# Three second-layer products of two units taken by a second level of fast products, and the order of the additions around them

## The chip, the cores and the metric

The kernel runs on one core of a Trainium2 chip. Its time is the device time of one execution in microseconds (us); the time before is the median of three executions, 630.69 us (630.52 to 631.08). The profile is of one more execution, and a profile starts at that execution's first instruction: places such as "at 597.34" are microseconds from there.

The engines are named as the profile names them. PE (TensorE) multiplies; PEld is its loading of weights. DVE (VectorE) and POOL (GpSimd) add and subtract, ACT (ScalarE) copies out of the accumulators and applies the activation, SP (SyncE) issues transfers. [...]

## The reference

A recurrent attention block gives 3072 tokens of 512 numbers; a two-layer network with a leaky activation follows. The second part is what matters here:

```python
def _moe_ref(x, w_in, w_out) -> np.ndarray:     # x 3072x512, w_in 512x2048, w_out 2048x512
    h = x @ w_in
    g = np.maximum(0.01 * h, h)
    return (g @ w_out).astype(np.float32)
```

Everything is float32. One product of the program is two matmul records in the profile[...].

## The kernel before

Tokens are worked in six chunks of 512 (c = 0 to 5), the 2048 hidden numbers in four units of 512 (u = 0 to 3). One step of the main loop is one unit of one chunk: n = 4(c - 2) + u runs from 0 to 15, and n = 12 to 15 are the last chunk. The first two chunks are done earlier, in another way.

Both layers use fast matrix products of the Strassen-Winograd kind. A 512x512 by 512x512 product is cut into 2x2 blocks and needs seven block products instead of eight, for a price of block sums before and after. "By two levels" means that each of the seven is cut again in the same way: seven products of quarter blocks instead of eight. The seven products of a block, each with half the columns, are PE work; the sums of operands and of results are DVE, POOL and ACT work.

Each step n does, in this order on PE:

1. `inner(n+1, 0)`: four of the seven first-layer products of the **next** unit, by two levels (28 products of 128x128, L1390). ACT copies results out of the accumulators (L1394 to L1402), DVE adds the others (`plus`, L619).
2. `trunk(n)`: three of the seven second-layer products of this unit, by one level only: "A" from block g0, "C" and "B" from differences of g, four products of 128x256 each (L1351). All three are accumulated **in PSUM** over the four units of a chunk, in banks 5, 7 and 4; `first` says when an accumulation starts anew (at u = 0).
3. `inner(n+1, 1)`: the other three first-layer products, by two levels (21 products of 128x128, L1390, in banks 0 to 3).
4. `leaf_steps(n)`: the other four second-layer products of this unit, by two levels (28 products of 128x128, L1311, in banks 0, 1, 2 and 6).

Around this lie the sums. `differences` (L622, four subtractions of 128x512 on DVE) makes the block differences of g for the second layer. `outer` combines the first-layer results to g (five additions of 128x512 in its second part), and `leaky` (L1432, ACT) activates them. `leaf_sums(n)` (L1290) makes the second-level operands of the four leaf blocks, four POOL instructions of 128x512. The results of `leaf_steps` go into the tile `w5` (`leaf_rooms()[5]`), or straight into the output tile `o` when u = 0, and `add_results` adds `w5` to `o` later: one DVE addition of 128x2048. When the trunk's accumulation is complete (last unit of a chunk), `trunk_taken` copies bank "A" into **the same tile** `w5` (ACT, L1359) and DVE adds "B", "C" and the sums to `o`. In the last chunk this happens at n = 14, because n = 15 uses `output` instead (L674), one level for all seven.

The order is written by hand. In step n the DVE queue gets, in this order: `add_results`, `differences(n)`, the result sums of `inner(n+1, 0)`, the first two additions of `outer(n+1)`, the trunk sums if there are any, the result sums of `inner(n+1, 1)`, the other additions of `outer(n+1)`, the result sums of `leaf_steps(n)`. The ACT queue at n = 14 gets the five copies of `inner(15, 0)`, then the copy L1359 of `trunk_taken`, then the five copies of `inner(15, 1)`.

How `inner` uses banks matters below: its products M1, M5, M4, M6 go to banks 0, 1, 2 and 3. M6 adds to the result of M1, which ACT first copies from bank 0 to bank 3 (L1394), so that M6, the fourth group, cannot start before that copy. `leaf_steps` has the same copy (L1315) with one group less between: there M2, the third group, reuses the bank that the copy reads.

Of the kernel before, what the change touches and what calls it, by code (L numbers as in the profile page):

```python
# [9 lines left out]
FP32 = mybir.dt.float32  # L10
# [6 lines left out]
ALU = mybir.AluOpType  # L17
# [5 lines left out]
def kernel(  # L23
# [56 lines left out]
    def unit(k):  # L80
        if k not in units:
            units[k] = unit_tile(k, f"w{k}")
        return units[k]
# [121 lines left out]
    def new_t(c, name):  # L205
        return work.tile([128, 3, 2, N], FP32, tag=f"t{c % 2}", name=name)

    def new_o(c, name="o"):
        return work.tile([128, 4, 2, N], FP32, tag=f"o{int(c > 0)}", name=f"{name}_{c}")
# [408 lines left out]
    def plus(out, a, b):  # L618
        return nc.vector.tensor_tensor(out=out, in0=a, in1=b, op=ALU.add)  # L619
# [186 lines left out]
    def tile_x(c):  # L806
        return work.tile([128, 4, 2, N], FP32, tag="x", bufs=2, name=f"x_{c}")
# [3 lines left out]
        return [x, new_t(c, f"t_{c}")]  # L811

    slot = [0]
    last_four = {}

    class Reversed:

# [6 lines left out]
    def new_g(c, u):  # L824
        i = slot[0]
        slot[0] = 1 - i
        both = work.tile([128, 7, 2, N], FP32, tag=f"g{i}", name=f"g_{c}_{u}")
        last_four[c, u] = both[:, 1:5]
        return u, both[:, 0:4], Reversed(both)

    def run(steps, at):
# [240 lines left out]
    def at_of(n):  # L1072
        return 2 + n // NU, n % NU
# [121 lines left out]
    def flat_of(part):  # L1195
        return part.rearrange("p i k n -> p (i k n)")
# [106 lines left out]

    def leaf_steps(n, moving):

        ps = [bank[i].rearrange("p (i n) -> p i n", i=4) for i in (0, 2, 1, 6)]
        results = leaf_results(n)
        leaf_weights[:] = of_unit.pop(n, leaf_weights)
        for m, q, j, s in LEAVES:
            for i, to in enumerate(TARGETS):  # L1310
                nc.tensor.matmul(ps[q][:, to], lhsT=leaf_weights[i][j], rhs=moving[s][:, i],  # L1311
                                 start=(i == 0 and m in ("M1", "M5", "M4")), stop=True,
                                 skip_group_check=True)
            if m == "M1":
                nc.scalar.copy(out=ps[3], in_=ps[0])  # L1315
            elif m == "M3":
                plus(results[:, :, 1], results[:, :, 1], ps[1])
            elif m == "M7":
                plus(results[:, :, 3], results[:, :, 3], ps[3])
            else:  # L1320
                nc.scalar.copy(out=results[:, :, {"M5": 3, "M4": 2, "M6": 1, "M2": 0}[m]],
                               in_=ps[q])
            yield

        plus(results[:, :, 2], results[:, :, 2], ps[3])
        plus(results[:, 2], results[:, 2], results[:, 3])
        if at_of(n)[1] > 0:
            unadded.append(lambda: plus(flat_of(os[at_of(n)[0]]), flat_of(os[at_of(n)[0]]),
                                        results.rearrange("p i q n -> p (i q n)")))

    unadded = []

# [11 lines left out]
    def trunk(n, part):  # L1344

        u, g, gd = part
        first = n == FIRST_LEAVES or u == 0
        for x, sa, rhs in (("A", 0, g[:, 0]), ("C", 4, gd[:, 0]), ("B", 5, gd[:, 1])):
            for i in range(2):
                for k in range(2):  # L1350
                    nc.tensor.matmul(room[x][:, i, :],  # L1351
                                     lhsT=block(2 * u + 1, sa)[:, k, ts(i, 128)],
                                     rhs=rhs[:, k, :], start=(first and i == 0 and k == 0),
                                     stop=(k == 1), skip_group_check=True)
# [61 lines left out]
    def outer(n, group, later=None):  # L1416

        if group == 0:
            gs[n] = new_g(*at_of(n))
        g = gs[n][1]  # L1420

        def to(i):
            return g[:, i].rearrange("p k (h n) -> p (k h) n", h=2)

        def leaky(i):
            if later is not None:
                later.append(lambda: leaky_now(i))
            else:
                leaky_now(i)

        def leaky_now(i):
            nc.scalar.activation(g[:, i], g[:, i], AF.Prelu, alpha=0.01)  # L1432

        if group == 0:
            plus(u2, u2, m1)
            return plus(to(1), u2, m5)
        plus(to(0), m1, m2)
        leaky(0)
        plus(to(1), to(1), m3)
        leaky(1)  # L1440
        plus(u2, u2, m7)
        plus(to(3), u2, m5)
        leaky(3)
        plus(to(2), u2, m4)
        leaky(2)

    def products(steps, n):

        for _ in range(n):
            next(steps, None)  # L1450
# [38 lines left out]
    for n in range(N2):  # L1489
        c, u = at_of(n)  # L1490
        more, visiting, leaves = n + 1 < N2, visits(n), by_leaves(n)
        scores_next = visiting and following(c + 1, 2 * u)
        last_leaves = leaves and (u == NU - 1 or n + 2 == N2)
        if u == 0 and not leaves:
            os[c] = new_o(c)
        if u > 0:
            add_results()
        if more:
            differences(*gs[n][1:])
            if n > 0:  # L1500
                begun = inner_steps(n + 1, 0, held=visiting)
                products(begun, 1)
            while held:
                held.pop()()
            products(begun, 7)
        part = gs.pop(n)
        behind = None
        if visiting:
            if u == 0:
                xs[c + 1] = new_x(c + 1)  # L1510
            joint_visit(c + 1, 2 * u)
            if leaves:
                load_rows(n, range(4)[2 if u == 0 else 0 :])
        elif leaves and u == NU - 1:
            behind = sums_of_x(c + 1, 1)
        if more:
            outer(n + 1, 0)
        if leaves and u == 0:
            finish_chunk(c - 1)
            os[c] = new_o(c)  # L1520
        if visiting and u == 1:
            behind = differences(*xs[c + 1])
        elif c + 1 < NC and u == 2:
            behind = sums_of_x(c + 1, 0)
        if leaves:
            moving = leaf_sums(n, behind if not scores_next else None)
            trunk(n, part)
            if visiting and not scores_next:
                fill(6, 2, start=False)
        else:  # L1530
            steps = output(c, os[c], [part], u == 0, u == NU - 1, room=room if more else last_room,
                           order=FUSED if more else LAST, held=held if more else None)
            products(steps, 3)
        if last_leaves:
            rest = trunk_taken(n, os[c])
            if n + 2 == N2:
                rest()
        if scores_next and leaves:
            scores_of_pair(*scores_next, [bank[i] for i in (1, 6, 2, 3)], second_mask_last=True)
        elif scores_next:  # L1540
            scores_of_pair(*scores_next)
        if visiting:
            load_unit(n + 2, 0)
        if not leaves:
            products(steps, 1)
        if n in (0, 1):
            keep.append(sums_of_rows(n))
        if n in (1, 2):
            keep.append(sums_of_rows(n + 1, nc.gpsimd))
        if more:  # L1550
            inner(n + 1, 1)
            if last_leaves and n + 2 < N2:
                rest()
            for i in range(2) if visiting else ():
                ahead(c + 2, 2 * u + i)
            if keep:
                keep.pop(0)()
            if not leaves:
                products(steps, 1)
            later = [] if leaves else None  # L1560
            outer(n + 1, 1, later)
        if leaves:
            leaf = leaf_steps(n, moving)
            last_one = n + 2 == N2
            for count, ready in ((1, 1), (1, 1), (2, 2)) if last_one else (
                    (4, 2 if u == NU - 1 else 3), (1, 2 if u == NU - 1 else 1)):
                products(leaf, count)
                for _ in range(ready):
                    later.pop(0)()
            if last_one:  # L1570
                differences(*gs[n + 1][1:])
            products(leaf, 8)
            if last_one:
                add_results()
        else:
            products(steps, 3)
        if by_leaves(n + 1) and n + 1 >= NU:
            if not visits(n + 1):
                load_rows(n + 1)
            elif u == NU - 1:  # L1580
                load_rows(n + 1, range(2))
# [92 lines left out]
```

## Time and profile before

| what | us | from |
|---|---|---|
| median of three executions | 630.69 | times |
| the profiled execution | 631.22 | times |
| its span, first to last instruction | 629.3 | page |
| PE busy | 622.8 (99%) | page, part 1 |
| DVE busy | 512.4 (81%) | page, part 1 |
| ACT busy | 281.4 (45%) | page, part 1 |
| POOL busy | 105.8 (17%) | page, part 1 |
| step n = 12 | 546.27 to 568.67 | timeline of PE |
| step n = 13 | 568.67 to 591.08 | timeline of PE |
| step n = 14 | 591.08 to 613.49 | timeline of PE |

The profiled execution took 631.22 us, 1.9 us more than its span; that difference lies outside the first and last instruction. It is 0.5 us above the median.

In the timeline a row is a run of like instructions: its start, how long it lasted, engine, line, operation, tiles written and read with their shapes, how many, and in brackets the engine's idle time before it and what ended that. A duration holds whatever the instruction waited for inside the engine, so the same shape can have different durations. In the names, the free blocks of the weight tiles are all called `w`: `w<-bank` at L1359 is the trunk copy into `w5`.

### The profile page before, as it was taken

Reading aid. Unit: us, or ns where it says so; the run is one execution under the profiler, and the core shown is the slowest. Engines: PE = TensorE matmul, PEld = TensorE weight load, DVE = VectorE, ACT = ScalarE, POOL = GpSimd, SP = SyncE. Lnnn points to the kernel's source line nnn. Section 1 sums busy time; section 2 is a strip of 40 time slices with the busy share of each in tenths; the row PEclk is TensorE's granted clock in tenths of the full one; section 3 lists DMA queues with packets and bytes.
Section 4 is the critical chain, followed back from the end, with each engine's and each line's share of the span. In section 5 each row is a group of like instructions: output and inputs, shape, how many; then the busy total and the mean of one; then the engine's idle time right before and its main releaser. Section 6 shows DMA issues by size and latency. Waiting matters only on the chain.

```text
span 629.3 us, 15220 instructions
## 1 busy us (share of the span) xinstructions
PE 622.8 (99%) x6375; PEld 572.2 (91%) x6375; DVE 512.4 (81%) x793; ACT 281.4 (45%) x543; POOL 105.8 (17%) x109
## 2 busy tenths in 40 slices
PE   8999999999999999999999999999999999999997
PEld 5888888888888889899999999999999999999996
DVE  5679769889979986679888968789968689977796
ACT  5876646446444114352433433534514435534540
POOL 2000000000010110105133052331250321333030
PEclk9999999999999999999999999999999999999999
DMA  8941425547782998396976996988478568678601
GB/s 328 405 143 34 126 75 193 167 133 252 243 296 73 347 333 272 101 339 190 349 228 215 283 333 240 324 280 280 150 257 298 156 216 281 209 264 278 205 1 68
DMA packets 105939, 140.99 MB, mean 224 GB/s; under 512 B 4488, under 2 KB 84232, under 8 KB 105872
## 3 DMA queue, kind: packets, MB, share of 16 engines
q1 hardware_dynamic: 105568, 139.41, 66.6%
q8 instruction: 50, 0.82, 0.5%
q10 hardware_dynamic: 304, 0.62, 0.3%
q14 instruction: 17, 0.14, 0.1%
HBM read 113.54 MB, written 26.48 MB: 222 GB/s over the span
## 4 chain that ended last, share of the span: by engine, by line
PE 94%; DVE 2%; ACT 1%; DMA 1%; issue 0%; SPq 0%; DVEq 0%; ACTq 0%
PE bank L1390 27%; PE bank L1311 12%; PE bank L1351 10%; PE bank L674 9%; PE C_h L674 4%; PE B_o L674 4%; PE A_h L674 4%; PE A_o L674 4%; PE C_o L674 4%; PE B_h L674 4%; PE D_o L674 2%; PE D_h L674 2%; PE d L695 2%; DMA raw<-in_weights_dram 1%; PE bank L371 1%; PE bank L453 1%
## 5 line engine op out<-in xcount | busy, mean ns | idle before, releaser
L619 DVE TENSOR_TENSOR made<-made,bank 128x512 f32<-128x512 f32 (+1 forms) x96 | 55.9, 617 | 39.8 <-PE bank L1390 35.9
L1390 PEld LDWEIGHTS bank<-x,wb 128*128 128x128 f32 x672 | 77.4, 192 | 1.2 <-ACT bank L1394 0.2
L1390 PE MATMUL bank<-x,wb 128*128 128x128 f32 x672 | 78.4, 276 | 0.0
L622 DVE TENSOR_TENSOR g<-g 128x512 f32<-128x512 f32 x96 | 64.0, 688 | 5.2 <-ACT g L1432 0.5
L1390 PE MATMUL bank<-x,wa 128*128 128x128 f32 x512 | 67.7, 275 | 0.0
L1394 ACT COPY bank<-bank 128x512 f32<-128x512 f32 (+1 forms) x32 | 16.6, 517 | 104.6 <-PE bank L1390 97.4
L1390 PEld LDWEIGHTS bank<-x,wa 128*128 128x128 f32 x512 | 62.7, 192 | 0.5 <-ACT made L1400 0.2
L1390 PE MATMUL bank<-t,wa 128*128 128x128 f32 x384 | 53.4, 275 | 0.0
L619 DVE TENSOR_TENSOR g<-made 128x512 f32<-128x512 f32 x64 | 49.0, 786 | 2.9
L1351 PE MATMUL bank<-g,w 128*128 128x256 f32 x216 | 48.5, 381 | 0.0
L1390 PEld LDWEIGHTS bank<-t,wa 128*128 128x128 f32 x384 | 48.0, 192 | 0.0
L1311 PE MATMUL bank<-g,w 128*128 128x128 f32 x368 | 47.0, 276 | 0.0
L1351 PEld LDWEIGHTS bank<-g,w 128*128 128x128 f32 x216 | 40.3, 190 | 5.4
L1311 PEld LDWEIGHTS bank<-g,w 128*128 128x128 f32 x368 | 43.8, 192 | 0.0
L1432 ACT ACTIVATE g<-g 128x512 f32<-128x512 f32 x64 | 37.7, 633 | 6.9 <-DVE g L619 6.9
L1290 POOL TENSOR_TENSOR x<-g 128x512 f32<-128x512 f32 x12 | 16.6, 1382 | 138.2 <-DVE t L622 40.1
L674 PE MATMUL bank<-g,w 128*128 128x256 f32 x168 | 38.0, 382 | 0.0
L674 PEld LDWEIGHTS bank<-g,w 128*128 128x128 f32 x168 | 31.3, 190 | 4.2
L619 DVE TENSOR_TENSOR o<-o,bank 128x512 f32<-128x512 f32 (+2 forms) x44 | 26.5, 633 | 9.8 <-ACT bank L788 4.2
L619 DVE TENSOR_TENSOR o<-o,w 128x2048 f32<-128x2048 f32 (+2 forms) x17 | 28.9, 1722 | 0.2
L674 PE MATMUL A_h<-x,w 128*128 128x256 f32 x112 | 26.6, 380 | 0.0
L163 POOL TENSOR_TENSOR in<-in,dec 128x512 f32<-128x512 f32 x2 | 2.4, 1232 | 139.7 <-DMA in<-in_kv_dram 139.7
(257 smaller groups left out, 1261.1 us busy)
## 6 DMA issues: line engine op xcount, KB each, us to landing
wa<-kept SPq DMA_DIRECT2D x16, 1344.0 KB, 8.7
w<-leaf_kept SPq DMA_DIRECT2D x44, 448.0 KB, 5.4
raw<-in_weights_dram SPq DMA_DIRECT2D x31, 512.0 KB, 4.4
wb<-kept SPq DMA_DIRECT2D x16, 896.0 KB, 6.0
wa<-kept SPq DMA_DIRECT2D x16, 448.0 KB, 4.7
wb<-kept SPq DMA_DIRECT2D x16, 448.0 KB, 6.8
out_dram<-o SPq DMA_DIRECT2D x23, 256.0 KB, 2.9
kept<-w SPq DMA_DIRECT2D x12, 448.0 KB, 5.7
```

What stands on the lines that cost most here:

```text
L371: nc.tensor.matmul(at[j][ts(h, 64), n, m, i], lhsT=x[ts(j, 64), 1, a, ts(h, 64)], rhs=x[ts(j, 64), 0, a, ts(h, 64)], start=(n == 0 and a = ...
L453: mm = nc.tensor.matmul(at[n][j][ts(i, 64), m, ts(h, 64)], lhsT=val[ts(h, 64), 2 * a + j], rhs=weights[j][ts(h, 64), n, m, i], start=(n == ...
L619: return nc.vector.tensor_tensor(out=out, in0=a, in1=b, op=ALU.add)
L622: return nc.vector.tensor_tensor(out=out, in0=a, in1=b, op=ALU.subtract)
L674: nc.tensor.matmul(to, lhsT=block(w, sa)[:, k, ts(i, 128)], rhs=rhs[:, k, a:z], start=(first and (i == 0 or split) and n == 0 and k == 0), ...
L695: nc.tensor.matmul(banks[r][:, i, :], lhsT=block(2 * u, r + 2 * kh)[:, k, ts(i, 128)], rhs=x[:, 2 * kh + th, k, :], start=(step == 0 and i ...
L1290: op = nc.gpsimd.tensor_tensor(out=out, in0=a, in1=b, op=ALU.subtract)
L1311: nc.tensor.matmul(ps[q][:, to], lhsT=leaf_weights[i][j], rhs=moving[s][:, i], start=(i == 0 and m in ("M1", "M5", "M4")), stop=True, skip ...
L1351: nc.tensor.matmul(room[x][:, i, :], lhsT=block(2 * u + 1, sa)[:, k, ts(i, 128)], rhs=rhs[:, k, :], start=(first and i == 0 and k == 0), s ...
L1390: nc.tensor.matmul(ps[q][:, i], lhsT=w[:, j, i], rhs=part_of(moving[i], s), start=(i == 0 and m in ("M1", "M5", "M4")), stop=True, skip_gr ...
L1394: nc.scalar.copy(out=ps[3], in_=ps[0])
L1432: nc.scalar.activation(g[:, i], g[:, i], AF.Prelu, alpha=0.01)
```

## The change

For n = 12 and 13, `trunk(n)` is replaced by `trunk_by_leaves`: its three products A, B and C are taken by two levels as well, as 21 products of 128x128 in banks 4 to 7, through the same routine that `leaf_steps` uses. The results no longer stay in PSUM: those of n = 12 go to a tile `all`, those of n = 13 to a tile `new`, and DVE adds `new` to `all`. Operand sums for them are made on POOL: `trunk_sums(n)` for the data, before the trunk, and `trunk_weights(n)` for the weights, in steps 9 and 12. After the second part of `outer(14)`, `trunk_all_taken` adds the three results to the four blocks of `o`, on POOL. The accumulation of the ordinary trunk starts anew at n = 14. In the last chunk `add_results` moves from before `differences(n)` to after the first part of `outer(n+1)`.

```diff
-        if u > 0:
+        if u > 0 and c < NC - 1:
             add_results()
...
+        if by_leaves_all(n):
+            trunk_moving = trunk_sums(n)
...
         if leaves and u == 0:
             finish_chunk(c - 1)
             os[c] = new_o(c)
+        elif more and c == NC - 1:
+            add_results()
...
             moving = leaf_sums(n, behind if not scores_next else None)
-            trunk(n, part)
+            if by_leaves_all(n):
+                trunk_by_leaves(n, trunk_moving)
+            else:
+                trunk(n, part)
...
+            if n == N2 - NU - 3:
+                trunk_weights(N2 - NU)
+            elif by_leaves_all(n) and by_leaves_all(n + 1):
+                trunk_weights(n + 1)
...
-            outer(n + 1, 1, later)
+            done = outer(n + 1, 1, later)
+            if by_leaves_all(n) and not by_leaves_all(n + 1):
+                trunk_all_taken(os[c], done)
...
-        first = n == FIRST_LEAVES or u == 0
+        first = n in (FIRST_LEAVES, N2 - 2) or u == 0
...
+    def by_leaves_all(n):
+        return N2 - NU <= n < N2 - 2
...
+    def trunk_weights(n):
...
+        for step in range(4):
+            for to, at in zip((slice(0, 1), slice(1, 3)), AT_ENDS):
...
+                nc.gpsimd.tensor_tensor(out=mine[step], in0=a, in1=b,
+                                        op=ALU.subtract if step else ALU.add)
...
+    def trunk_sums(n):
...
+        for step in range(4):
+            for to, at in zip((slice(0, 1), slice(1, 3)), AT_ENDS):
...
+                nc.gpsimd.tensor_tensor(out=out, in0=a, in1=b, op=ALU.subtract)
...
+    def trunk_by_leaves(n, moving):
...
+        to = end_rooms["all" if at_of(n)[1] == 0 else "new"]
+        ps = [bank[i][:, 0 : 3 * C].rearrange("p (i n) -> p i n", i=3) for i in (4, 5, 7, 6)]
+        products(quartered(ps, trunk_tiles.pop(n), moving, flat_of(to).rearrange(
+            "p (i q n) -> p i q n", i=3, q=4), range(3)), 8)
         if at_of(n)[1] > 0:
+            plus(end_rooms["all"], end_rooms["all"], to)
+
+    def trunk_all_taken(o, behind):
+
+        a, ab, abc = (end_rooms["all"][:, i] for i in range(3))
+        for out, x, y in ((ab, ab, a), (abc, abc, ab), (o[:, 0], o[:, 0], a),
+                          (o[:, 1], o[:, 1], abc), (o[:, 2], o[:, 2], ab),
+                          (o[:, 3], o[:, 3], abc)):
+            op = nc.gpsimd.tensor_tensor(out=out, in0=x, in1=y, op=ALU.add)
+            if behind is not None:
+                tc.add_manual_dep(op.ins, behind.ins.name, IN_ORDER, reason="one port for both")
+                behind = None
```

`quartered` is the old body of `leaf_steps` (its products, ACT copies and three DVE additions out of PSUM), now with the banks, weights, operands and targets as parameters; the addition of `ps[3]` to the third result, which followed the products before, stands in it.

More of the change, by code (lines that the diff above doesn't have):

```diff
@@ L813 @@
     slot = [0]
-    last_four = {}
+    last_four, last_seven = {}, {}
     class Reversed:
@@ L828, in new_g @@
         last_four[c, u] = both[:, 1:5]
+        last_seven[c, u] = both
         return u, both[:, 0:4], Reversed(both)
@@ L1304, in leaf_steps, with quartered @@
     def leaf_steps(n, moving):
-        ps = [bank[i].rearrange("p (i n) -> p i n", i=4) for i in (0, 2, 1, 6)]
         results = leaf_results(n)
         leaf_weights[:] = of_unit.pop(n, leaf_weights)
+        ps = [bank[i].rearrange("p (i n) -> p i n", i=4) for i in (0, 2, 1, 6)]
+        yield from quartered(ps, leaf_weights, [[x[:, i] for x in moving] for i in range(4)],
+                             results, TARGETS)
+        plus(results[:, 2], results[:, 2], results[:, 3])
+        if at_of(n)[1] > 0:
+            unadded.append(lambda: plus(flat_of(os[at_of(n)[0]]), flat_of(os[at_of(n)[0]]),
+                                        results.rearrange("p i q n -> p (i q n)")))
+    def quartered(ps, weights, moving, results, targets):
         for m, q, j, s in LEAVES:
-            for i, to in enumerate(TARGETS):
-                nc.tensor.matmul(ps[q][:, to], lhsT=leaf_weights[i][j], rhs=moving[s][:, i],
+            for i, to in enumerate(targets):
+                nc.tensor.matmul(ps[q][:, to], lhsT=weights[i][j], rhs=moving[i][s],
                                  start=(i == 0 and m in ("M1", "M5", "M4")), stop=True,
@@ L1319, in leaf_steps @@
                 plus(results[:, :, 3], results[:, :, 3], ps[3])
+                plus(results[:, :, 2], results[:, :, 2], ps[3])
             else:
@@ L1323, in leaf_steps, with quarters_of @@
             yield
-        plus(results[:, :, 2], results[:, :, 2], ps[3])
-        plus(results[:, 2], results[:, 2], results[:, 3])
-        if at_of(n)[1] > 0:
-            unadded.append(lambda: plus(flat_of(os[at_of(n)[0]]), flat_of(os[at_of(n)[0]]),
-                                        results.rearrange("p i q n -> p (i q n)")))
+    AT_ENDS = (slice(0, 1), slice(5, 7))
+    end_rooms = {}
+    def by_leaves_all(n):
+        return N2 - NU <= n < N2 - 2
+    def quarters_of(x):
+        return [x[:, :, k, ts(h, C)] for k in range(2) for h in range(2)]
@@ new lines, in trunk_weights @@
+    def trunk_weights(n):
+        if "r" not in end_rooms:
+            end_rooms["r"] = new_o(0, "r")
+        r = flat_of(end_rooms["r"])[:, 0 : 12 * C].rearrange("p (j i n) -> p j i n", j=4, i=3)
+        blocks = unit(2 * at_of(n)[1] + 1)
+        for step in range(4):
+            for to, at in zip((slice(0, 1), slice(1, 3)), AT_ENDS):
+                a11, a21, a12, a22 = quarters_of(blocks[:, at])
+                mine = [r[:, j, to] for j in range(4)]
+                a, b = ((a21, a22), (mine[0], a11), (a12, mine[1]), (a11, a21))[step]
+                nc.gpsimd.tensor_tensor(out=mine[step], in0=a, in1=b,
+                                        op=ALU.subtract if step else ALU.add)
+        trunk_tiles[n] = [[blocks[:, at, 0, 0:C], blocks[:, at, 1, 0:C], blocks[:, at, 1, C:]]
+                          + [r[:, j, i] for j in range(4)] for i, at in enumerate((0, 5, 6))]
@@ new lines @@
+    trunk_tiles = {}
+    def trunk_sums(n):
+        if "sums" not in end_rooms:
+            end_rooms["sums"] = [work.tile([128, 2, HP, C], FP32, tag=tag, bufs=AHEAD,
+                                           name=f"trunk_{tag}") for tag in ("qk", "kv", "kv")]
+        made = [x.rearrange("p s a t -> p (s a) t")[:, 0:3] for x in end_rooms["sums"]]
+        both = last_seven[at_of(n)]
+        for step in range(4):
+            for to, at in zip((slice(0, 1), slice(1, 3)), AT_ENDS):
+                b11, b12, b21, b22 = quarters_of(both[:, at])
+                mine = [x[:, to] for x in made]
+                out, a, b = ((mine[0], b12, b11), (mine[1], b22, mine[0]), (mine[2], b21, mine[1]),
+                             (b12, b22, b12))[step]
+                nc.gpsimd.tensor_tensor(out=out, in0=a, in1=b, op=ALU.subtract)
+        moving = []
+        for i, at in enumerate((0, 5, 6)):
+            b11, b12, b21, b22 = (x[:, 0] for x in quarters_of(both[:, at : at + 1]))
+            moving.append([b11, b21, *(x[:, i] for x in made), b22, b12])
+        return moving
@@ new lines, in trunk_by_leaves @@
+    def trunk_by_leaves(n, moving):
+        if "all" not in end_rooms:
+            end_rooms["all"] = new_t(0, "trunk_all")
+            end_rooms["new"] = tile_x("trunk")[:, 0:3]
+        to = end_rooms["all" if at_of(n)[1] == 0 else "new"]
+        ps = [bank[i][:, 0 : 3 * C].rearrange("p (i n) -> p i n", i=3) for i in (4, 5, 7, 6)]
+        products(quartered(ps, trunk_tiles.pop(n), moving, flat_of(to).rearrange(
+            "p (i q n) -> p i q n", i=3, q=4), range(3)), 8)
+        if at_of(n)[1] > 0:
+            plus(end_rooms["all"], end_rooms["all"], to)
@@ L1443, in outer @@
         leaky(3)
-        plus(to(2), u2, m4)
+        done = plus(to(2), u2, m4)
         leaky(2)
+        return done
     def products(steps, n):
```

## The prediction, made before the changed kernel ran

> **What bounds the kernel now.** First the page's busy shares, then the chain that ended last (94% PE), then the timelines of PE, ACT, DVE and POOL over the last chunk. PE is never idle in steps 12 to 14, so only its own work, or a wait put in its way, moves the end.
>
> ```profile
> PE 622.8 (99%) x6375; PEld 572.2 (91%) x6375; DVE 512.4 (81%) x793; ACT 281.4 (45%) x543; POOL 105.8 (17%) x109
> ```
>
> Then PE's timeline in step 14 (start, length, engine, line, what):
>
> ```profile
> 597.34 5.35 PE L1351 MATMUL bank<-g,w 128*128 128x256 f32 x24
> 602.52 4.85 PE L1390 MATMUL bank<-x,wb 128*128 128x128 f32 x42
> 607.21 1.06 PE L1311 MATMUL bank<-g,w 128*128 128x128 f32 x8
> ```
>
> Starts follow without a gap: a trunk takes 602.52 - 597.34 = 5.18 us, the 21 products after it 607.21 - 602.52 = 4.69 us.
>
> ```profile
> 599.26 0.59 ACT L1359 COPY w<-bank 128x512 f32<-128x512 f32 x1 [2.93 <-PE bank L1351]
> 603.38 0.46 ACT L1394 COPY bank<-bank 128x384 f32<-128x384 f32 x1 [3.53 <-PE bank L1390]
> ```
>
> ACT waits for PE in both rows. The second is the copy that M6 of `inner(15, 1)` needs. M6 is due 3 x 0.67 us after 602.52, at 604.53; the copy ends at 603.84. PE has 0.7 us to spare there.
>
> ```profile
> 592.60 0.69 DVE L619 TENSOR_TENSOR w<-w 128x512 f32<-128x512 f32 x1
> 593.33 2.29 DVE L619 TENSOR_TENSOR o<-o,w 128x2048 f32<-128x2048 f32 x1
> 595.54 1.41 DVE L622 TENSOR_TENSOR g<-g 128x512 f32<-128x512 f32 x2
> 597.40 1.29 DVE L622 TENSOR_TENSOR g<-g 128x512 f32<-128x512 f32 x2 [0.46 <-DVE g L622]
> 598.61 1.88 DVE L619 TENSOR_TENSOR made<-made,bank 128x512 f32<-128x512 f32 x3
> 600.59 1.45 DVE L619 TENSOR_TENSOR made<-made 128x512 f32<-128x512 f32 x1
> 602.15 1.57 DVE L619 TENSOR_TENSOR g<-made 128x512 f32<-128x512 f32 x1
> ```
>
> DVE works here almost without a pause from 592 to 608: in step 14 it has no slack. The row at 593.33 is `add_results`, which frees `w5` six microseconds before L1359 writes it.
>
> ```profile
> 600.23 1.27 POOL L1290 TENSOR_TENSOR wb<-g,x 128x512 f32<-128x512 f32 x1
> 601.58 1.59 POOL L1290 TENSOR_TENSOR more_room<-g,wb 128x512 f32<-128x512 f32 x1
> 603.13 1.72 POOL L1290 TENSOR_TENSOR g<-g 128x512 f32<-128x512 f32 x1
> ```
>
> Read these against the last two DVE rows. POOL's first ends at 601.50, and DVE's addition issued at 600.59 ends at 602.04: it ran in the 0.54 us after. POOL's next ends 1.13 us after that (603.17), DVE's next 0.55 us after that (603.72), POOL's last 1.13 us later (604.85). The two take strict turns.
>
> [...] additions with a PSUM operand keep their 0.60 us spacing beside POOL, those out of SBUF lose 0.8 to 0.9 us each. [...] The clock here is granted in full in steps 12 to 14[...].
>
> **The change part by part.** Times are of before unless said otherwise.
>
> 1. PE: 24 records of 128x256 become 42 of 128x128, twice: 2 x (5.18 - 4.69) = -0.98 us. But the third group, M2 into bank 4, must wait for the copy of M1. In the rows of `inner(15, 1)` the copy ends 603.84 - 602.52 = 1.32 us after the first product starts; add about 0.12 to the next product (leaf copy to M2: 608.87 to 608.99) and M2 starts at 1.45 instead of 1.34. That returns 0.1 us per unit (bounds 0 and 0.3). Sum about -0.75 us.
>
> 2. POOL's operand sums. One 128x128 takes 0.46 and one 128x256 0.73 us (single rows of L1249 at 311.50 and 312.84), so four pairs are 4.8 us. `trunk_weights` in steps 9 and 12 and `trunk_sums` in 12 and 13 are 4 x 4.8 us on a queue that is 17% busy. They collide with DVE, not with time on PE: laid out by turns, the last activation's input in steps 9 and 12 is ready within 0.3 us of need. In step 13 DVE's differences end 1.5 us late, and the last operand of M7, whose third part PE needs about 4.3 us after the trunk's start, comes about 0.2 us late. I take 0.25 us, bounds 0 and 1.
>
> 3. DVE's added work in steps 12 and 13: three additions of 128x384 out of PSUM (0.55 each, 1.65 us) each, plus `all + new` of 128x1536 (about 1.7 us, three quarters of 2.29). They fall where DVE waits for PE: 2.2 us before 561.99 and 4.4 us before 584.40. Hidden; if POOL's turns use up that cover, DVE starts the next sums up to 1 us late, inside the slack of their banks.
>
> 4. So PE enters `inner(15, 1)` 0.5 us early, at 602.0, and M6 is due at 604.0.
>
> 5. `trunk_all_taken`: six POOL instructions of 128x512, 7.7 us, from the end of `outer(14)` (about 588.9) to at best 596.7. They lie on DVE's busiest stretch. In turns, with 1.15 us for POOL and 0.55 for DVE: DVE's `w<-w` (592.1 now) goes behind POOL's third, to 593.5; the four differences go behind the fourth, fifth and sixth, to 595.2, 596.9, 598.65 and 599.25. That is 0.5 us later than before (598.70), although the 2.29 us of `add_results` no longer stand ahead: POOL's turns eat what the move freed.
>
> 6. `leaf_sums(14)` starts at 599.4. DVE's three sums out of PSUM end at 601.1; `made+made` goes behind POOL's second, to 602.55; `g<-made` behind its third, to 604.25 (before: 603.72). Only now comes `add_results`, behind POOL's fourth (605.4), with 2.15 us (2.29 free; behind a turn, the row of 556.40 ended 2.15 us after POOL): 607.55.
>
> 7. The new wait. L1359 writes `w5`, so it now waits for that: it runs from 607.6 to 608.2 instead of 599.26. Behind it in ACT's queue stand the five copies of `inner(15, 1)`. L1394 ends at about 608.65 instead of 603.84, and M6 starts at 608.75, due 604.0. PE stands still for 4.75 us. The other copies follow 0.5 us apart, ahead of M3 and M7; no second stall.
>
> 8. Afterwards everything keeps its distance from PE: `leaf_steps(14)` starts near 611.4 instead of 607.21, and DVE, after the five trunk additions (3.8 us from 607.5), begins the next sums at 611.3 beside it, as in before (607.29). The tail is shifted: +4.2 us. What was saved on PE is lost inside the stall.
>
> Against the profile's own time this is a span of about 633.5 and an execution of 635.4; the median stands 0.5 us below the profiled execution, so 630.7 + 4.2 = 634.9 us. [...]
>
> **Rivals.** What a measurement of this kernel can tell from no change is about 0.2%, 1.3 us, so 629.4 to 632.0 counts as the same.
>
> A. *Strict turns don't hold[...].* Then the differences end at 595.6, the sums out of PSUM (PE has them at 596.2) at 598.1, `g<-made` at 599.5; `trunk_all_taken`, pushed back, ends at 599.3, `add_results` at 601.8, and L1394 is in time. The saving stays: 630.0 to 630.2 us, not slower. It decides from the point where `add_results` ends before 602.6. Against it: every pair at 600 to 605 took turns. 10%.
>
> B. *Half the collision.* If `trunk_all_taken` cost DVE nothing, `g<-made` would end near 601.9, still behind `leaf_sums`, `add_results` at 604.1, L1394 at 605.2, a stall of 1.2 us: 631.4 us. This is the least the moved addition costs if POOL's four turns of before remain. One or two turns fewer than in 5 and 6 give 632.5 to 633.7. 15%, half of it within 0.2%.
>
> C. *The stall also costs the clock.* [...] 636.6 us. 17%.
>
> D. *The change isn't made as told.* The changed program's order has the 21 products in both units and the copy of L1359 waiting for DVE ahead of the five copies. About nothing.
>
> **How the numbers follow.** The likeliest, 634.9, has 58%, with its own range 633.5 to 636.3 (one turn of 1.2 us either way and the bounds of 1 and 2). With C above and part of B below, the range for 8 in 10 is 631.6 to 637.4. Even the whole saving, 0.98 us, is under 1.3 us, so faster by over 0.2% needs something that I don't see: 0.03. Same: A and half of B, 0.15. Slower: 0.82.
>
> **What would show it.** L1359's successor ends its wait on DVE near 607.6, with ACT idle for some 10 us before it; PE has one gap of 4 to 5 us inside `inner(15, 1)`, before its fourth group; the DVE addition of 128x2048 ends just before. PE's trunks in steps 12 and 13 take 4.7 to 5.0 us. I am wrong if PE shows no gap there, if that addition ends before 602.6, or if gaps lie elsewhere, at M7 of the trunk in step 13 above all.

## The result, and the profile after

The changed kernel takes 637.43 us (median of four executions, 636.78 to 637.93), beside 630.61 us before (four executions, 630.50 to 631.08): a ratio of 1.0106, 95% interval 1.0089 to 1.0124. It is slower by 6.8 us. The profiled execution took 637.61 us with a span of 635.7 us, 6.4 us more than before's span.

First PE's timeline in step 14 of the changed kernel. The columns are start, length, engine, line, what, and in brackets idle time and its end. L1426 is the ordinary trunk (L1351 before), L1465 is `inner` (L1390), L1321 the products by two levels (L1311).

```profile
596.78 5.35 PE L1426 MATMUL bank<-g,w 128*128 128x256 f32 x24
601.96 2.17 PE L1465 MATMUL bank<-x,wb 128*128 128x128 f32 x18
608.31 5.24 PE L1465 MATMUL bank<-x,wb 128*128 128x128 f32 x24 [4.18 <-ACT bank L1469]
613.39 1.06 PE L1321 MATMUL bank<-g,w 128*128 128x128 f32 x8
```

The row of 42 records of before is torn in two. The first three groups (18 records) start at 601.96, 0.56 us earlier than before. The fourth is due 18 x 0.1117 us later, at 603.97, and starts at 608.31: 4.34 us of waiting. And the 24 records after it take 613.39 - 608.31 = 5.08 us, where 24 x 0.1117 = 2.68 us are due: 2.40 us more. What follows it, `leaf_steps(14)`, starts 6.18 us later than before (613.39, before 607.21), and that is the whole loss of the span up to the last 0.2 us.

What PE waited for stands in ACT's timeline (L1434 is the trunk copy, L1359 before; L1469 is the copy for M6, L1394 before):

```profile
595.19 0.59 ACT L1477 COPY made<-bank 128x512 f32<-128x512 f32 x1 [0.25 <-PE bank L1465]
607.29 0.59 ACT L1434 COPY w<-bank 128x512 f32<-128x512 f32 x1 [11.51 <-DVE o L619]
607.77 0.49 ACT L1469 COPY bank<-bank 128x384 f32<-128x384 f32 x1
608.18 0.48 ACT L1471 COPY made<-bank 128x384 f32<-128x384 f32 x1
```

ACT stands still for 11.51 us and waits for a DVE addition to `o`. The copy that waits is eight microseconds late; the next two follow at once, because their products had long been done. What held DVE is read from its timeline and POOL's:

```profile
592.05 1.24 DVE L619 TENSOR_TENSOR w<-w 128x512 f32<-128x512 f32 x1
593.20 5.71 DVE L622 TENSOR_TENSOR g<-g 128x512 f32<-128x512 f32 x4
598.84 1.87 DVE L619 TENSOR_TENSOR made<-made,bank 128x512 f32<-128x512 f32 x3
600.81 1.45 DVE L619 TENSOR_TENSOR made<-made 128x512 f32<-128x512 f32 x1
602.36 1.57 DVE L619 TENSOR_TENSOR g<-made 128x512 f32<-128x512 f32 x1
603.86 3.35 DVE L619 TENSOR_TENSOR o<-o,w 128x2048 f32<-128x2048 f32 x1
```

```profile
588.87 2.63 POOL L1401 TENSOR_TENSOR trunk_all<-trunk_all 128x512 f32<-128x512 f32 x2 [4.42 <-DVE g L619]
591.47 6.30 POOL L1401 TENSOR_TENSOR o<-o,trunk_all 128x512 f32<-128x512 f32 x4
```

The four differences (L622) take 5.71 us beside POOL's four additions to `o`; the first two and the last two took 1.41 and 1.29 us before. The moved addition stands last, starts at 603.86, waits for one more turn of POOL and ends at 607.21, 3.35 us after its start where 2.29 us stand before. The additions with a bank among their inputs (598.84) are as fast as ever: 1.87 us for three, 1.88 before.

The chain that ended last shows the same in one view. Before, it ran through PE alone from 599.88 to 624.06. Now it leaves PE at 590.7 and comes back at 608.3 (start, length, what; pieces of under 0.1 us left out):

```profile
592.05 1.24 DVE w L619
...
598.24 0.68 DVE g L622
598.91 1.80 DVE made L619 x3
...
602.36 1.57 DVE g L619
603.93 3.28 DVE o L619
...
607.29 0.59 ACT w L1434
607.88 0.39 ACT bank L1469
...
608.31 5.24 PE bank L1465 x24
```

The slow records are explained by the clock, from busy times by stretch (the stretch, its length, the busy time of PE, PEld, DVE, ACT and POOL, the granted clock, DMA share and GB/s):

```profile
601.96:606.40 4.44, 2.17 (x19) 1.98 (x17) 4.34 (x3) 0.00 (x0) 3.10 (x2) 0.99 0.00 0
606.40:613.16 6.76, 4.85 (x22) 4.85 (x23) 5.04 (x7) 2.71 (x6) 0.00 (x0) 0.50 0.00 0
613.39:619.68 6.29, 6.29 (x59) 6.29 (x57) 5.72 (x10) 4.69 (x9) 0.00 (x0) 1.00 0.01 3
```

The clock is full until about 606.3, half until about 613.2 (by its own record, from which the stretches were chosen), and full again; before, it is 1.00 in each of steps 12 to 14. It fell while PE stood still. PE worked 4.85 us at half speed, which is 2.4 us of lost work: the 2.40 us of above. Of the other executions only the mean clock over the whole span is on record. The 6.8 us at half give 0.995 for the profiled execution; the other three have 0.993, 0.997 and 0.996, where ten executions of before, run beside the first four experiments, have 0.999 or 1.000. So the clock fell in each of the four, in two of them for less time than here; where in the span it fell the means do not say, and three of the 25 executions of before beside the last two runs have 0.996 or 0.997 too. The 2.40 us are measured in the profiled execution alone.

### The profile page after: what moved, and what is told of

It is laid out like the page before. It is cut to its first block, busy times and chain, and to the rows that moved or that the text cites. A ratio compares the mean times of both kernels' runs of the same rounds, so it can differ in the third digit from the quotient of the medians.

```text
span 635.7 us, 15365 instructions
## 1 busy us (share of the span) xinstructions
PE 624.9 (98%) x6411; PEld 574.6 (90%) x6411; DVE 526.0 (83%) x800; ACT 285.7 (45%) x553; POOL 141.9 (22%) x147
## 4 chain that ended last, share of the span: by engine, by line
PE 91%; DVE 4%; ACT 2%; DMA 1%; issue 1%; POOL 0%; DVEq 0%; ACTq 0%; SPq 0%; POOLq 0%
PE bank L1465 26%; PE bank L1321 13%; PE bank L674 9%; PE bank L1426 7%; PE C_h L674 4%; PE B_o L674 4%; PE A_h L674 4%; PE A_o L674 4%; PE C_o L674 4%; PE B_h L674 4%; PE D_o L674 2%; PE D_h L674 2%; PE d L695 2%; PE bank L453 1%; PE bank L436 1%; DVE g L622 1%
## 5 line engine op out<-in xcount | busy, mean ns | idle before, releaser
L1465 PE MATMUL bank<-x,wb 128*128 128x128 f32 x672 | 80.9, 281 | 4.2 <-ACT bank L1469 4.2
L1465 PEld LDWEIGHTS bank<-x,wb 128*128 128x128 f32 x672 | 79.6, 197 | 5.5 <-ACT bank L1469 4.5
L622 DVE TENSOR_TENSOR g<-g 128x512 f32<-128x512 f32 x96 | 68.7, 736 | 4.8 <-ACT g L1507 0.5
L1465 PE MATMUL bank<-x,wa 128*128 128x128 f32 x512 | 67.8, 275 | 0.0
L1465 PEld LDWEIGHTS bank<-x,wa 128*128 128x128 f32 x512 | 62.7, 192 | 0.6 <-ACT made L1475 0.2
L1469 ACT COPY bank<-bank 128x512 f32<-128x512 f32 (+1 forms) x32 | 16.6, 520 | 89.5 <-PE bank L1465 82.3
L619 DVE TENSOR_TENSOR g<-made 128x512 f32<-128x512 f32 x64 | 51.0, 817 | 2.9
L1465 PE MATMUL bank<-t,wa 128*128 128x128 f32 x384 | 53.3, 275 | 0.0
L1321 PE MATMUL bank<-g,w 128*128 128x128 f32 x392 | 50.8, 277 | 0.0
L1465 PEld LDWEIGHTS bank<-t,wa 128*128 128x128 f32 x384 | 48.0, 192 | 0.0
L1321 PEld LDWEIGHTS bank<-g,w 128*128 128x128 f32 x392 | 46.8, 192 | 0.4 <-ACT o L1332 0.2
L674 PE MATMUL bank<-g,w 128*128 128x256 f32 x168 | 38.0, 382 | 0.0
L1426 PE MATMUL bank<-g,w 128*128 128x256 f32 x168 | 37.8, 382 | 0.0
L1426 PEld LDWEIGHTS bank<-g,w 128*128 128x128 f32 x168 | 31.4, 190 | 4.2
L674 PEld LDWEIGHTS bank<-g,w 128*128 128x128 f32 x168 | 31.3, 190 | 4.2
L417 POOL MEMSET between<- 128x1 f32 x16 | 1.9, 118 | 131.9 <-PE bank L453 103.9
```

The lines of the kernel that those rows point to most:

```text
L674: nc.tensor.matmul(to, lhsT=block(w, sa)[:, k, ts(i, 128)], rhs=rhs[:, k, a:z], start=(first and (i == 0 or split) and n == 0 and k == 0), ...
L1321: nc.tensor.matmul(ps[q][:, to], lhsT=weights[i][j], rhs=moving[i][s], start=(i == 0 and m in ("M1", "M5", "M4")), stop=True, skip_group_c ...
L1426: nc.tensor.matmul(room[x][:, i, :], lhsT=block(2 * u + 1, sa)[:, k, ts(i, 128)], rhs=rhs[:, k, :], start=(first and i == 0 and k == 0), s ...
L1465: nc.tensor.matmul(ps[q][:, i], lhsT=w[:, j, i], rhs=part_of(moving[i], s), start=(i == 0 and m in ("M1", "M5", "M4")), stop=True, skip_gr ...
```

## The experiments

The theory: POOL's turns push DVE back, the moved addition ends late, ACT's queue waits behind one copy, PE waits for the next copy, and the clock falls on top. The rivals: the move alone is at fault; or POOL's turns are; or the copy's wait is only where a lateness shows that would cost the same without it; or the slow records have another cause than the clock. Each run is given beside the executions of before on the same chip: ten with a median of 630.62 us for the first four runs, 25 with 630.87 us for the last two.

**Without the six additions.**

```diff
             done = outer(n + 1, 1, later)
-            if by_leaves_all(n) and not by_leaves_all(n + 1):
-                trunk_all_taken(os[c], done)
```

> The six GpSimd additions of the three results to the output are left out, so the output lacks three of the second-layer products of the last chunk's first two units; all else as in the changed kernel. Theory[...]: the moved addition ends near 604.1, the stall is 1.2 to 1.6 us[...], 631.2 to 632.0 us. Rival (the place of the moved addition alone makes the loss): the stall stays over 3 us, 635 us or more.

Measured: 632.73 us, ratio 1.0033 (1.0022 to 1.0044); the median lies 0.7 us above the range named. In the trace:

```profile
602.36 2.28 DVE L619 TENSOR_TENSOR o<-o,w 128x2048 f32<-128x2048 f32 x1
```

```profile
605.75 2.94 PE L1465 MATMUL bank<-x,wb 128*128 128x128 f32 x24 [1.00 <-ACT bank L1469]
```

The moved addition ends at 604.64 instead of 607.21, PE's fourth group was due at 604.59 and starts at 605.75: 1.16 us. The 24 records then take 2.78 us, so the clock stays full (its mean over the span is 0.999). The six additions thus make some 3.2 us of the waiting and, through the clock, the other 2.4. Two things in its profile bear on the missed range: this run also lost 0.27 us in `leaf_steps(14)`, and it did not have the early start of the changed kernel's profiled execution (0.2 us later than before at the start of the last chunk's steps, against 0.46 us earlier).

**Without the move.**

```diff
-        if u > 0 and c < NC - 1:
+        if u > 0:
             add_results()
...
-        elif more and c == NC - 1:
-            add_results()
```

> Only the move of the addition of w5 to the output is undone: it stands ahead of the differences again. Theory: the copy in step 14 is free, but the addition now waits for the last GpSimd addition to the output, which ended at 597.8, with the differences behind it in VectorE's queue; the differences that the trunk's second product needs at 598.5 come at 600.9 or later, and VectorE stays 4 us late to the end: a stall inside the trunk of step 14 of 2 to 3 us and more later, 633 to 636.5 us. Rival (the move was the whole fault): 630 to 631 us.

Measured: 633.89 us, ratio 1.0053 (1.0038 to 1.0068). DVE's and PE's timelines:

```profile
596.54 2.29 DVE L619 TENSOR_TENSOR o<-o,w 128x2048 f32<-128x2048 f32 x1 [3.61 <-POOL o L1401]
598.75 2.81 DVE L622 TENSOR_TENSOR g<-g 128x512 f32<-128x512 f32 x4
```

```profile
599.49 3.72 PE L1426 MATMUL bank<-g,w 128*128 128x256 f32 x16 [1.17 <-DVE g L622]
...
613.68 1.16 PE L1321 MATMUL bank<-g,w 128*128 128x128 f32 x8 [1.28 <-ACT w L1332]
615.26 1.13 PE L1321 MATMUL bank<-g,w 128*128 128x128 f32 x8 [0.42 <-ACT w L1332]
```

The time lies in the theory's range, and the waits are where it put them: the addition now waits 3.61 us for POOL's last addition to the same tile, and PE waits for the differences, inside the trunk. The size there was missed: PE lost 1.44 us in the trunk, not 2 to 3, and 2.21 us in `leaf_steps(14)`. POOL's four additions to `o` took 5.40 us instead of 6.30 and so ended earlier, at 596.51: DVE's differences no longer stood beside them. So the move was not the whole fault, but a part of it: undoing it alone takes 3.5 us off the changed kernel's time, and 3.3 us of loss stay. With the move PE waited 4.34 us instead of 3.65 us in all, and the clock fell on top (2.40 us); here it stayed full (mean 0.999).

**Another tile for the copy.**

```diff
-        a, ab, abc = (flat_of_k(leaf_results(n)[:, i]) for i in range(3))
+        if n + 2 == N2:
+            a, ab, abc = (end_rooms["new"][:, i] for i in range(3))
+        else:
+            a, ab, abc = (flat_of_k(leaf_results(n)[:, i]) for i in range(3))
```

> The trunk copy of step 14 goes into the tile that step 13's trunk results used, no longer into w5, so it does not wait for the moved addition; all else as in the changed kernel. Theory (the wait of that one copy holds the five copies behind it): the copy runs near 599, there is no gap before the fourth group of the first-layer products, and the clock stays full there. VectorE is as late as before, though (the moved addition still ends near 607, the next result sums begin near 611 with the products done at 606.5), so the last output waits for its differences instead: 631.5 to 633.5 us. Rival (VectorE's lateness alone makes the loss, the copy is only where it shows): 635 us or more.

Measured: 635.85 us, ratio 1.0084 (1.0069 to 1.0099). The theory's range fails and the rival's number holds. The copies of `inner(15, 1)` are on time, and `leaf_steps(14)` starts without a gap at 606.85. Inside it PE waits (its timeline, then a stretch with the granted clock):

```profile
611.86 1.13 PE L1321 MATMUL bank<-more_room,w 128*128 128x128 f32 x8 [1.25 <-DVE made L619]
614.69 3.68 PE L1321 MATMUL bank<-g,w 128*128 128x128 f32 x16 [1.70 <-ACT w L1332]
```

```profile
614.70:618.20 3.50, 3.50 (x16) 3.50 (x17) 3.27 (x6) 2.96 (x6) 0.00 (x0) 0.51 0.00 0
```

The moved addition still ends at 607.4, the result sums start at 611.17, and `leaf_steps` waits twice: for a bank that DVE has not read yet, and for copies that stand in ACT's queue behind activations which wait for DVE (5.03 us, until 613.54). In the profiled execution the clock falls here too: it is half for 3.4 us from 614.8 on, and the last 16 records take 3.52 us where 1.79 are due. In one of the four executions it did not fall (mean clock 1.000), and that one still took 635.40 us. The copy into `w5` is the first place where DVE's lateness reaches PE, not the only one. Freeing the queue gained only 1.6 of the 6.8 us, while the engine that it had waited for stayed late.

**PE kept busy during the wait.**

```diff
         for m, q, j, s in INNER:
+            if m == "M6" and group == 1 and n == N2 - 1:
+                for _ in range(18):
+                    fill(6)
```

> The changed kernel with 18 products on a constant tile (128x512, bf16[...], into a bank that is free) put before the fourth group of the first-layer products of step 15, in the place where TensorE stands still. Theory (the stall costs twice: 4.3 us of waiting and 2.4 us of half clock after it): the 24 records after the wait take 2.7 us in place of 5.1, the granted clock stays full, 635.0 us. Rival (the records after the wait are slow because their operands come late): 637.4 us, as without them.

Measured: 635.90 us, ratio 1.0087 (1.0070 to 1.0104). PE's timeline, then the stretch with the granted clock:

```profile
604.16 4.05 PE L707 MATMUL bank<-mask 128*128 128x512 bf16 x18
608.48 2.94 PE L1468 MATMUL bank<-x,wb 128*128 128x128 f32 x24 [0.28 <-ACT bank L1472]
611.26 1.06 PE L1321 MATMUL bank<-g,w 128*128 128x128 f32 x8
```

```profile
606.60:611.26 4.66, 4.38 (x32) 3.30 (x31) 3.92 (x6) 2.71 (x6) 0.00 (x0) 1.00 0.00 0
```

The wait is as long as in the changed kernel (the fourth group starts at 608.48), but the 24 records take 2.78 us and the clock stays at 1.00. The span is 633.6 us, 2.1 us shorter; the medians differ by 1.5 us. The median is 0.9 us above the 635.0 expected, of which its trace shows 0.27 us in `leaf_steps(14)` and another 0.36 us in step 12 (0.76 us lost there, 0.40 in the changed kernel's profile). The mean clock is 0.999 or 1.000 in three of the four executions and 0.997 in the other. The fourth group started as late as in the changed kernel and its records were fast, so the slow records were the clock's.

**Sums at the end.** Both faults are taken out: no additions on POOL after `outer(14)`, no move. As in the two runs above, the edit takes out the call of `trunk_all_taken` and sets `add_results` back; what is new in it:

```diff
+    def end_sums():
+        sums = [end_rooms["all"][:, i] for i in range(3)]
+        for to, x in zip(sums, "ABC"):
+            plus(to, to, room[x])
+        plus(sums[1], sums[1], sums[0])
+        plus(sums[2], sums[2], sums[1])
+    def end_added(o):
+        a, ab, abc = (end_rooms["all"][:, i] for i in range(3))
+        for i, x in ((0, a), (3, abc), (2, ab), (1, abc)):
+            nc.gpsimd.tensor_tensor(out=o[:, i], in0=o[:, i], in1=x, op=ALU.add)
...
             if n + 2 == N2:
-                rest()
+                end_sums()
...
         if not leaves:
             products(steps, 1)
+        if not more:
+            end_added(os[c])
```

> Both parts of step 14 that cost time are gone: the addition of w5 stands ahead of the differences again, and the six GpSimd additions after outer(14) are not made. Instead VectorE adds banks A, B and C of step 14 to the three kept results and sums them up (five additions, no copy by ScalarE, no use of w5), and GpSimd adds the four sums to the output in the last step, where VectorE's additions all read PSUM. Theory: step 14 runs as before the change, no stall there; the two trunks save 0.35 us each as they did in the changed kernel, and step 12 still loses some 0.5 us to the copies that wait for the output transfers of the chunk before: 630.2 to 630.8 us. Rival (the operand sums on GpSimd in steps 9 to 13 cost more than they save, so two levels do not pay in any order): over 631 us.

Measured: 630.83 us (thirteen executions) beside 630.87 us, ratio 1.0002 (0.9994 to 1.0010), at the upper end of the theory's range. Against before, then, the changed kernel lost 6.8 us, without the six additions it lost 2.1, without the move 3.3, and with neither, their sums made elsewhere, nothing that can be measured. The two parts together cost more than the sum of both alone. Step 14 has no gap, and POOL's additions lie in the last step, where DVE's all read PSUM: 4.95 us for four, 1.24 each, nobody waits. Counted from the start of the last chunk's steps, PE gains 0.35 us in each of the two trunks and loses 0.61 and 0.19 us in step 12 and right behind it. ACT's timeline tells why:

```profile
565.71 1.56 ACT L1332 COPY o<-bank 128x512 f32<-128x512 f32 x3 [2.56 <-DMA out_dram<-o]
```

The copies of step 12 go into `o`, and that tile still holds the output of the chunk before. Its four transfers landed after up to 4.9 us in the changed kernel, where the same wait stands with 2.34 us, and after up to 2.8 us before the change, where no copy waited for them.

**Two tiles swapped.**

```diff
-            os[c] = new_o(c)
+            os[c] = tile_x("o_last") if c == NC - 1 else new_o(c)
...
-            end_rooms["new"] = tile_x("trunk")[:, 0:3]
+            end_rooms["new"] = new_o(1, "trunk")[:, 0:3]
```

> As the run with sums at the end, and two tiles swapped: the last chunk's output lies in the tile that held the products' new results, and these lie in the tile of the output before, so that the copies of step 12 into the output do not wait for the transfers of the chunk before. Theory: the loss of 0.5 us in step 12 goes, the whole 0.7 us of the two trunks stay: 629.7 to 630.1 us. Rival (step 12 loses its time to GpSimd's turns on VectorE, the transfer only ended last): as without the swap, 630.2 to 630.8 us.

Measured: 630.41 us (thirteen executions) beside 630.87 us, ratio 0.9993 (0.9983 to 1.0003). By its time the theory's range (629.7 to 630.1) was missed, and the number lies in the rival's. The trace has to decide between them. The same copies in ACT's timeline:

```profile
563.59 0.59 ACT L1332 COPY x_o_last<-bank 128x512 f32<-128x512 f32 x1 [0.32 <-PE bank L1321]
564.51 0.59 ACT L1332 COPY x_o_last<-bank 128x512 f32<-128x512 f32 x1 [0.34 <-PE bank L1321]
```

They wait for PE alone, and the loss in and behind step 12 is gone, while POOL's additions in step 12 take as long as without the swap. So the wait for the transfer was the cause of the loss in step 12, as the theory has it. PE enters the last step 1.13 us earlier than before, of which 0.44 us were there when the last chunk began: the stretch that was changed is 0.69 us shorter. By the time of the whole execution the interval still includes no change, so this version is faster by its trace and not by its times; the difference is smaller than its executions differ among themselves (629.68 to 632.45 us).

## Why the prediction was right, and where it was short

The sign, the place and the mechanism up to PE's wait were right; the time was short by 2.5 us (634.9 forecast, 637.43 measured). The median lies at the very top of the range for 8 in 10 (637.4) and above the likeliest case's own range (633.5 to 636.3). What came was rival C in kind, which had 17% and named 636.6.

- Step 1, PE's saving: -0.75 us forecast, 2 x -0.35 us measured. M2 waits for the copy of M1 in both trunks: it starts 0.72 and 0.71 us after its predecessor, where 0.67 is due, and takes 0.77 us itself. That is 0.15 us per unit where 0.1 was forecast, inside the bounds.
- Step 2, POOL's operand sums, 0.25 us with bounds of 0 and 1: PE lost 0.60 us in and right behind step 12 of the changed kernel, inside the bounds, but not at M7 of step 13 as forecast. It was the output transfers of the chunk before, which the prediction did not look at. The swap of tiles, which removed the loss, shows it.
- Step 3, DVE's added work, hidden as forecast: the result sums of `inner(14, 1)` start at 583.84, half a microsecond after DVE had nothing left to do.
- Step 4: PE enters `inner(15, 1)` 0.56 us early, 0.5 forecast; but 0.46 us of this were there when the last chunk began. Only 0.10 us are the change's.
- Steps 5 to 7, the turns and the wait: the differences end at 598.92 (599.25 forecast), `g<-made` at 603.93 (604.25), the moved addition at 607.21 (607.55), the copy starts at 607.29 (607.6), M6 at 608.31 (608.75), after 4.34 us (4.75). Turns hold throughout this stretch, so rival A falls. Rival B's case was run by leaving the additions out: 1.16 us of waiting against 1.2, though at 632.73 us, not 631.4.
- Step 8 failed: "leaf_steps(14) starts near 611.4". It starts at 613.39. The term is the clock, put at nothing in the likeliest case and at 1.7 us in rival C (636.6 less 634.9), which was the author's estimate: the profile of before has no fall (mean clock 1.000). The mean clock is lower than before's in all four executions, and in the profiled one the fall cost 2.40 us. There PE's last product before the fall ended near 604.1 and the clock fell at 606.3, some 2.2 us later. It stayed half for 6.8 us, of which PE worked 4.85 us. What sets the moment of the fall and its length was not shown.

With 634.9 + 2.4 the sum comes to 637.3. The chain of the forecast was right and its last term missing. That the sum meets the median so closely is partly luck: PE's wait was forecast 0.4 us too long, and before's profiled execution lay 0.6 us above its median, the changed kernel's only 0.2 us above.

## What to carry to other kernels

Before moving an addition behind other work, list who writes the tile that it reads: here one late buffer halted ACT's queue for 11.51 us, and the two copies behind, whose products had long been done, started only 0.5 and 0.9 us after the one that waited. Work for GpSimd cost VectorE nothing here beside additions that read PSUM (1.87 us for three, with GpSimd at work beside them at 598.84 and without it at 508.63 of before). Those with two SBUF inputs were held up. The four differences took 5.71 us while three of GpSimd's additions ended beside them, and 2.81 us with none (without the move); the moved addition took 3.35 us with one and 2.28 us with none (without the six additions). That is about 1.0 to 1.1 us for each GpSimd instruction of 128x512, which took 1.28 us itself at 588.87, with no such addition beside it. With the sums at the end such work stood beside additions out of PSUM: GpSimd's four took 4.95 us, VectorE's five of 128x256 took 2.01 us, as they do without it, and nobody waited; there such work went free. And the halt of TensorE has to be priced with the half clock that followed it: 2.4 us after a wait of 4.3 us.

## What the runs showed of the hardware that was not expected

- The clock fell 2.2 us into the wait of the changed kernel, at 606.3, and stayed half for 6.8 us. Two short waits were enough as well: with another tile for the copy, PE stood still from about 610.6 to 611.9 and from 613.0 to 614.7, with 1.1 us of products between, and the clock was half from 614.8 to 618.2 (in one of four executions it stayed full). A single wait of 1.2 us (without the six additions), and waits of 1.2, 1.3 and 0.4 us, the first two 14 us apart (without the move), did not lower it in the profiles, and the mean clocks of all eleven executions of these two runs are 0.999 or 1.000. The rule behind this was not worked out and stays open.
- 18 products on a constant tile in the gap held the clock at full in the profiled execution; they cost no visible time there, as the wait was longer (4.32 us) than they were (4.05 us).
- An output transfer that nothing in the change touches became late enough to hold up copies in every profile taken that keeps the two tiles as they were. With the tiles swapped it still lands after 5.0 us, and nobody waits. What made it land that late instead of after 2.8 us was not tried and stays open.
